# The last quarter of two weight tiles by itself, and the last outputs made in two steps

## The chip, the cores and the metric

The kernel runs on one core of one Trainium2 chip. The time is that of the device for one execution, in microseconds (us). Five engines work side by side, each through its own list of instructions in order: TensorE (PE; PEld are its weight loads), VectorE (DVE), ScalarE (ACT), GpSimd (POOL) and SyncE (SP). Transfers are issued by an engine's queue (here SP's and POOL's) and carried out by 16 DMA engines.

## What is computed

Attention with a feature map of exponentials (its output is x) is followed by a spectral mix over the sequence: the first 64 frequencies of x are multiplied with complex 512 x 512 matrices, transformed back and added to x, and a small network with ReLU is added to the sum.

```
def _moe_ref(x, w_r, w_i, w_ch):
    X = np.fft.rfft(x, axis=1)
    Y = np.zeros_like(X)
    Xr, Xi = (np.real(X[:, :n_modes]), np.imag(X[:, :n_modes]))
    Yr = np.einsum('bmd,mde->bme', Xr, w_r) - np.einsum('bmd,mde->bme', Xi, w_i)
    Yi = np.einsum('bmd,mde->bme', Xr, w_i) + np.einsum('bmd,mde->bme', Xi, w_r)
    Y[:, :n_modes] = Yr + 1j * Yi
    y = np.fft.irfft(Y, n=S, axis=1)
    u = x + y
    return (u + np.maximum(u @ w_ch, 0.0)).astype(np.float32)
```

x is 8 x 576 x 512, w_r and w_i are 64 x 512 x 512 each in float32 (134 MB together), the output is 8 x 576 x 512 in float32 (9.44 MB).

## The kernel before

**Weights.** The 64 modes stand in 8 groups of 8 (o = 0 to 7), the 512 input features in 4 groups of 128 (g = 0 to 3). One weight tile, (g, w) with w = 2 o + i, holds 8 modes by 128 features by 512 of w_r (i = 0) or w_i (i = 1). `wload` (line 348) brings it by one transfer on POOL's queue that also turns float32 into bfloat16: 2 MB are read, 1 MB is put down. In the tile, [128, 4, 2, 512], partition 2p + a holds modes 4a to 4a + 3, so index 3 of the second axis is modes 3 and 7. The tiles live in the pool `pw` of 9 buffers (line 83); `next_w` issues the next one of the list `wq`, in the order of lines 359 to 362: the groups o = 6 and 7 of g = 1 to 3 come last, and the very last are (3, 14) and (3, 15).

**Mix.** `mix` (line 472) multiplies a tile with the spectrum XT on TensorE. A matmul has 32 columns of weights (two parts, two signs and 8 batches of one mode), so four modes fill 128 output rows in PSUM: rows 0 to 31 are modes 0 and 4 of the tile (j = 0), rows 96 to 127 modes 3 and 7 (j = 3). For o = 7 the 512 output columns lie as two halves in two banks. Groups 0 to 5 are summed in `yacc`, the late groups through g = 1 to 3 in PSUM, with the part of g = 0 added from `late`.

**The end of a group.** When tile (3, 2 o + 1) is through (lines 1001 to 1058): `yst` is y of this group, 128 x 512 in bfloat16; it is transposed on TensorE, copied to `yT` and multiplied with w_ch (`wchb`) to z, copied to `zst`. Groups 0 to 6 are parked and laid out (`park`, `lay`) for the sums over many modes. `put` (line 838) copies yst and zst of groups 6 and 7 into the tile `yl`, 16 partitions at a time, twice each (128 KB a copy): for o = 6 by POOL's queue, for o = 7 by SP's.

**Sums and outputs.** `todo` is a list of closures that `fill` runs between the tiles: products x w_ch (`Channels`) and the inverse transforms of groups 0 to 6 (`Absorb`, two PSUM banks each, from the pools `pst` and `psa` of four banks each, lines 603 to 612). The 36 output pieces of 128 x 512 leave in 18 pairs (`pairs`, line 633). A pair has a side e, which ScalarE copies to `rl` (with or without ReLU; GpSimd may add x to it), and a side d in two banks (`pp`), which VectorE adds to it into `of`; one side is made of y, the other of z. A pair marked straight (third entry in the table) takes the part of group 7 from yst or zst themselves, the others take groups 6 and 7 from `yl`. `plan` (line 653) is the order of TensorE's instructions at the end, written by hand: a word has the side, then b (base: x or x w_ch by an identity matmul), s or l (the sum), the pair's name and perhaps which half. Words without a pair are marks: `until` (line 943) plays the plan up to one. A pair whose sums are all issued is added and stored by SP in the order of the table; the first one leaves in two halves.

All instructions keep the order of the program on their engine (the class InOrder), so line 37 stands for nearly all of them, and the profile is read by tile names.

Of the kernel before, what the change touches and what calls it, by code (L numbers as in the profile page):

```python
# [11 lines left out]
BF16 = mybir.dt.bfloat16  # L12
# [31 lines left out]
def kernel(  # L44
# [303 lines left out]
    def wload(g, w):  # L348
        wt = home(g, w)
        o, i = w // 2, w % 2  # L350
        w = (moe_w_r, moe_w_i)[i]
        pool.dma_start(
            wt.rearrange("p m r e -> p m (r e)"),
            w[MG * o:MG * o + MG, g * 128:(g + 1) * 128, :].rearrange(
                "m (p r) e -> p m (r e)", r=2))
        return wt
# [4 lines left out]
    order = list(wq)  # L361
    wq.remove((0, 5))
# [3 lines left out]
    def next_w(n):  # L366
        for _ in range(n):
            if wq:
                key = wq.pop(0)
                wts[key] = wload(*key)  # L370
# [101 lines left out]
    def mix(g, w, wt, XT, bank):  # L472
# [6 lines left out]
        n = 1 if w < 14 or not late else 2  # L479
        if first:  # L480
            pys[w // 2] = [bank() for _ in range(n)]
        for h, py in enumerate(pys[w // 2]):
            cols = slice(DMODEL // n * h, DMODEL // n * (h + 1))
            for r in range(2):
                for j in range(4):
                    pe.matmul(
                        py[32 * j:32 * j + 32, 0:DMODEL // n],
# [126 lines left out]
    def banks(dt=F32):  # L614
# [18 lines left out]
    pairs = {  # L633
        "00": (((0, 0), (0, 1)), True, False, True),
        "02": (((0, 2), (0, 3)), True, False, False),
        "06": (((0, 6), (0, 7)), True, True, True),
        "04": (((0, 4), (0, 5)), False, False, False),
        "34": (((3, 4), (3, 5)), False, False, True),
        "30": (((3, 0), (3, 1)), False, False, False),
        "n0": (((0, 8), (1, 8)), False, False, True),  # L640
        "14": (((1, 4), (1, 5)), False, False, False),
        "10": (((1, 0), (1, 1)), False, False, True),
        "24": (((2, 4), (2, 5)), False, False, True),
        "22": (((2, 2), (2, 3)), False, False, False),
        "32": (((3, 2), (3, 3)), False, False, True),
        "26": (((2, 6), (2, 7)), False, False, False),
        "12": (((1, 2), (1, 3)), False, False, False),
        "n1": (((2, 8), (3, 8)), False, False, False),
        "20": (((2, 0), (2, 1)), False, False, True),
# [314 lines left out]
    while mixq:  # L964
# [30 lines left out]
        if g == NG - 1 and i == 1:  # L995
# [15 lines left out]
            for h in range(2):  # L1011
                if end:
                    until(f"T{h}")
# [78 lines left out]
```

## Time and profile before

| what | value |
|---|---|
| time of three runs | 431.33 us median (430.72 to 431.49) |
| the profiled execution, its own time | 432.54 us |
| its span, first to last instruction | 430.7 us |
| mean granted TensorE clock | 0.928 |
| busy PE, DVE, ACT, POOL | 324.0, 302.4, 299.8, 123.8 us |
| read and written in HBM | 163.64 MB, 9.44 MB |
| weight transfers | 58 into wt of 1 MB, 27 us from issue to landing |
| output stores | 17 of 512 KB (4.6 us to landing), 2 of 256 KB (2.5 us) |

The span is what the profile covers; around it lies 1.84 us of the profiled execution's own time. Busy shares are averages over stages with different limits. The page's 40 slices of 10.8 us show which resource is full in which stage:

```profile
PE   1677577678787776876877767867899789985992
DMA  9999999999999999999999999999999999997697
GB/s 216 210 211 211 238 213 237 226 223 237 240 210 236 214 237 238 238 210 239 213 239 221 226 244 228 212 212 212 212 211 212 212 211 212 211 212 158 230 392 305
```

A digit is the busy share of a slice in tenths, GB/s is what the DMA engines put down.

### The profile page before, as it was taken

How to read it: one execution, taken by the hardware profiler on the slowest of the kernel's cores; microseconds unless marked ns; L12 is line 12 of the kernel's file. 1: busy time of each engine (PE TensorE's matmuls, PEld its weight loads, DVE VectorE, ACT ScalarE, POOL GpSimd, SP SyncE). 2: the span in 40 equal slices, each digit the busy share in tenths (PEclk: the TensorE clock that was granted, in tenths of full speed). 3: DMA queues.
4: the chain of work that ended last, by engine and by line, in shares of the span. 5: the costliest groups of instructions: out<-in, count | busy, mean ns of one | idle time of the engine just before them, and what ended most of it. 6: DMA issues, size and time to landing. Idle time of an engine off the chain costs nothing.

```text
span 430.7 us, 10131 instructions
## 1 busy us (share of the span) xinstructions
PE 324.0 (75%) x4208; PEld 197.8 (46%) x4255; DVE 302.4 (70%) x594; ACT 299.8 (70%) x487; POOL 123.8 (29%) x161
## 2 busy tenths in 40 slices
PE   1677577678787776876877767867899789985992
PEld 1345455446454553654645545543355333332320
DVE  6758767766677767878877878868644656972684
ACT  3787886877879779888878779766644346661872
POOL 6232132022321312321222321221012035750882
PEclk9979898889988989998988989899899999998998
DMA  9999999999999999999999999999999999997697
GB/s 216 210 211 211 238 213 237 226 223 237 240 210 236 214 237 238 238 210 239 213 239 221 226 244 228 212 212 212 212 211 212 212 211 212 211 212 158 230 392 305
DMA packets 49687, 97.71 MB, mean 227 GB/s; under 512 B 2282, under 2 KB 11626, under 8 KB 49642
## 3 DMA queue, kind: packets, MB, share of 16 engines
q0 software_dynamic: 45088, 85.27, 101.3%
q1 hardware_dynamic: 4394, 11.73, 7.2%
q8 instruction: 33, 0.54, 0.5%
q14 instruction: 12, 0.10, 0.1%
q10 hardware_dynamic: 160, 0.07, 0.1%
HBM read 163.64 MB, written 9.44 MB: 402 GB/s over the span
## 4 chain that ended last, share of the span: by engine, by line
PE 38%; ACT 28%; DVE 19%; DMA 7%; issue 5%; POOL 2%; ACTq 0%; DVEq 0%; POOLq 0%
PE one L37 14%; PE pt L37 13%; ACT AQ L37 12%; PE two L37 8%; ACT AB L37 8%; DVE m L37 7%; DMA wt<-in_moe_w_i_dram 7%; ACT qT L37 3%; ACT XT L37 3%; DVE xs L37 3%; PE pp L37 2%; DVE xw L37 2%; DVE of L37 2%; DVE mk L37 1%; DVE yacc L37 1%
## 5 line engine op out<-in xcount | busy, mean ns | idle before, releaser
L37 ACT ACTIVATE AQ<-two 128x1024 bf16<-128x1024 f32 x64 | 80.7, 1351 | 2.0 <-PE two L37 1.9
L37 ACT ACTIVATE AB<-two 128x1024 bf16<-128x1024 f32 x64 | 62.9, 1058 | 3.3 <-DVE mk L37 3.0
L37 ACT CAST xw<-pt 128x512 bf16<-128x512 f32 x54 | 31.6, 585 | 37.1 <-PE pt L37 36.3
L37 DVE TENSOR_REDUCE m<-two 128x8 f32<-128x1024 f32 x32 | 39.1, 1223 | 22.4 <-PE two L37 22.4
L37 DVE TENSOR_REDUCE mk<-two 128x8 f32<-128x1024 f32 x32 | 38.9, 1219 | 9.2 <-PE two L37 9.2
L37 PE MATMUL pt<-wchb,xT 128*128 128x512 bf16 x135 | 37.1, 388 | 8.3 <-DVE xT L37 2.4
L37 POOL DMA_DIRECT2D wt<-in_moe_w_i_dram x28 | 21.0, 751 | 76.3 <-PE pt L37 36.5
L37 PE MATMUL two<-w2blk,qT 128*128 128x256 bf16 x128 | 24.1, 322 | 24.1 <-ACT AQ L37 13.6
L37 DVE TENSOR_TENSOR va<-vn,ee 128x1152 bf16<-128x1152 f32 x32 | 42.0, 1355 | 0.0
L37 POOL DMA_DIRECT2D wt<-in_moe_w_r_dram x30 | 22.4, 747 | 55.9 <-PE one L37 28.2
L37 PEld LDWEIGHTS <-xs 128*128 128x128 bf16 x624 | 31.1, 102 | 12.7 <-issue 6.0
L37 ACT COPY qT<-one 128x512 bf16<-128x512 bf16 (+1 forms) x32 | 19.0, 642 | 23.0 <-PE one L37 22.9
L37 PEld LDWEIGHTS <-qT 128*128 128x128 bf16 x144 | 15.3, 109 | 38.9 <-issue 34.8
L37 PE MATMUL two<-mT,minus 96*128 96x512 bf16 x64 | 26.5, 414 | 2.9 <-issue 0.9
L37 POOL DMA_DIRECT2D kb<-in_k_dram x16 | 11.4, 712 | 60.1 <-PE one L37 53.4
L37 PEld LDWEIGHTS <-XT 128*32 128x32 bf16 x560 | 15.8, 148 | 28.0 <-issue 18.3
L37 DVE TENSOR_TENSOR xs<-one,rd 128x384 bf16<-128x384 f32 x48 | 26.8, 557 | 1.6
L37 PE MATMUL one<-kvz,AQ 128*128 128x65 bf16 x512 | 25.9, 203 | 1.0 <-ACT qT L37 0.8
L37 PEld LDWEIGHTS <-AQ 128*128 128x128 bf16 x512 | 23.2, 104 | 7.2 <-issue 3.0
L37 PE MATMUL one<-wt,XT 128*32 128x512 bf16 x272 | 23.8, 438 | 3.4 <-ACT XT L37 3.4
L37 POOL TENSOR_TENSOR rl<-rl,xs 128x512 f32<-128x512 f32 x18 | 20.3, 1159 | 19.3 <-ACT rl L37 18.7
L37 PE MATMUL two<-w2blk,kT 128*128 128x256 bf16 x128 | 21.1, 293 | 5.1 <-ACT AB L37 5.1
(151 smaller groups left out, 725.4 us busy)
## 6 DMA issues: line engine op xcount, KB each, us to landing
wt<-in_moe_w_r_dram POOLq DMA_DIRECT2D x30, 1024.0 KB, 26.6
wt<-in_moe_w_i_dram POOLq DMA_DIRECT2D x28, 1024.0 KB, 27.7
out_dram<-of SPq DMA_DIRECT2D x17, 512.0 KB, 4.6
vn<-in_v_dram POOLq DMA_DIRECT2D x13, 576.0 KB, 24.4
kb<-in_k_dram POOLq DMA_DIRECT2D x16, 288.0 KB, 19.2
qb<-in_q_dram POOLq DMA_DIRECT2D x16, 288.0 KB, 18.3
xs<-in_moe_w_i_dram POOLq DMA_DIRECT2D x2, 1024.0 KB, 23.0
vn<-in_v_dram SPq DMA_DIRECT2D x2, 576.0 KB, 4.7
```

The lines of the kernel that those rows point to most:

```text
L37: ins = f(*args, **kwargs)
```

## The change

- The last two tiles, (3, 14) and (3, 15), come in parts: modes 0 to 2 and 4 to 6 in two transfers of 384 KB each (one for each parity of the partitions), and at the very end of the list, modes 3 and 7 of both tiles in one transfer of 256 KB each.
- `mix` takes the modes to do. For these two tiles the main loop does j = 0 to 2, and a new function `finish` does j = 3 when the rest is there. For group 7 it uses three banks: rows 0 to 95 in two halves of the columns as before, and the rows of j = 3 in a third bank as four column blocks of 128, each in its own group of 32 rows. So a matmul of j = 3 has 128 columns.
- `finish` makes yst, yT and z of rows 0 to 95 first, puts j = 3 of tile 14 and then of tile 15 between the z matmuls, copies the third bank to `y3`, transposes it once, moves its four blocks into rows 96 to 127 of yst (two copies on VectorE, two on GpSimd), and makes z of those rows with 8 matmuls of 256 columns.
- `put` of group 6 goes to SP's queue instead of POOL's.
- Four pairs instead of three are straight (04 is new); the order of pairs, which of them use GpSimd, and the plan are new; the first three pairs are stored in halves.
- `Absorb` takes its banks from `psa` alone while group 7 holds its three banks. For the groups before 7, y is added in one instruction of 512 columns instead of two of 256, yT is one tile, and the transposes' banks are taken one after the other.

```diff
@@ -345,20 +345,29 @@
             return pw.tile([128, 4, 2, DMODEL], BF16, name="wt", tag="wt")
         return t.rearrange("p (m r e) -> p m r e", m=4, r=2)
 
-    def wload(g, w):
-        wt = home(g, w)
-        o, i = w // 2, w % 2
-        w = (moe_w_r, moe_w_i)[i]
-        pool.dma_start(
-            wt.rearrange("p m r e -> p m (r e)"),
-            w[MG * o:MG * o + MG, g * 128:(g + 1) * 128, :].rearrange(
-                "m (p r) e -> p m (r e)", r=2))
+    parted = [(NG - 1, w) for w in range(2 * NO - 2, 2 * NO)]
+
+    def wload(g, w, rest=False):
+        wt = wts[g, w] if rest else home(g, w)
+        to = wt.rearrange("p m r e -> p m (r e)")
+        src = (moe_w_r, moe_w_i)[w % 2][
+            MG * (w // 2):MG * (w // 2) + MG, g * 128:(g + 1) * 128, :].rearrange(
+                "m (p r) e -> p m (r e)", r=2)
+        if rest:
+            pool.dma_start(to[:, 3], src[:, 3::4])
+        elif (g, w) in parted:
+            for a in range(2):
+                pool.dma_start(to.rearrange("(p a) m e -> a p m e", a=2)[a, :, 0:3],
+                               src[:, 4 * a:4 * a + 3])
+        else:
+            pool.dma_start(to, src)
         return wt
 
     wts = {}
     wq = [(g, mg) for g in range(NG) for mg in range(12 if g else 2 * NO)]
     wq += [(g, 2 * o + i) for o in (6, 7) for g in range(1, NG) for i in range(2)]
     order = list(wq)
+    wq += [(*key, True) for key in parted]
     wq.remove((0, 5))
     wq.insert(1, (0, 5))
     mixq = []
@@ -367,7 +376,9 @@
         for _ in range(n):
             if wq:
                 key = wq.pop(0)
-                wts[key] = wload(*key)
+                wts[key[:2]] = wload(*key)
+                if len(key) > 2 and wq:
+                    next_w(1)
 
     scr = xs[:, 1].rearrange("p b n d -> p (b n d)").bitcast(F32)
     wpf = scr[:, 1920:2048]
@@ -469,22 +480,30 @@
                                   op0=ALU.mult, op1=ALU.add)
     pys = {}
 
-    def mix(g, w, wt, XT, bank):
+    def mix(g, w, wt, XT, bank, modes=range(4)):
 
         o, i = w // 2, w % 2
         late = g > 0 and o > 5
         first, last = i == 0 and (not late or g == 1), i == 1 and (not late or g == NG - 1)
         if late and g == 1:
             XT, o = XTb[0], o - 2
-        n = 1 if w < 14 or not late else 2
+        end = late and w >= 2 * NO - 2
         if first:
-            pys[w // 2] = [bank() for _ in range(n)]
-        for h, py in enumerate(pys[w // 2]):
-            cols = slice(DMODEL // n * h, DMODEL // n * (h + 1))
-            for r in range(2):
-                for j in range(4):
+            pys[w // 2] = [bank() for _ in range(3 if end else 1)]
+        py = pys[w // 2]
+        for r in range(2):
+            for j in modes:
+                at = py[0][32 * j:32 * j + 32]
+                parts = [(at, slice(0, DMODEL))]
+                if end and j < 3:
+                    parts = [(py[h][32 * j:32 * j + 32, 0:256], slice(256 * h, 256 * h + 256))
+                             for h in range(2)]
+                elif end:
+                    parts = [(py[2][32 * c:32 * c + 32, 0:128], slice(128 * c, 128 * c + 128))
+                             for c in range(4)]
+                for at, cols in parts:
                     pe.matmul(
-                        py[32 * j:32 * j + 32, 0:DMODEL // n],
+                        at,
                         lhsT=XT[:, i, r, :, :, :, 4 * o + j].rearrange("p t x b -> p (t x b)"),
                         rhs=wt[:, j, r, cols], start=(first and r == 0), stop=(last and r == 1),
                     )
@@ -631,31 +650,31 @@
     eye = pb.tile([128, 128], F32, name="eye", bufs=1)
 
     pairs = {
+        "02": (((0, 2), (0, 3)), True, False, False),
         "00": (((0, 0), (0, 1)), True, False, True),
+        "04": (((0, 4), (0, 5)), True, False, True),
+        "06": (((0, 6), (0, 7)), True, True, False),
+        "32": (((3, 2), (3, 3)), False, True, False),
+        "14": (((1, 4), (1, 5)), False, False, True),
...
     }
     plan = (
-        "db02 db00 mix eb020 T0 T1 es000 z0a z0b z1 es001 es020 eb06 es061 "
-        "eb021 es060 ds00 es021 ds02 eb04 el34 ds06 el04 db04 eln0 dl04 eb30 db34 el30 dl34 db30 dl30 el10 "
-        "eb14 dbn0 dln0 el14 db14 el24 dl14 eb22 db10 dl10 el32 el22 db24 dl24 eb26 db22 el20 "
-        "dl22 db32 el26 dl32 eb12 db26 dl26 el12 ebn1 db12 eln1 dl12 dbn1 dln1 el16 eb36 db20 "
-        "el36 dl20 db36 dl36 db16 dl16").split()
+        "db00 db02 mix T es000 z eb020 es020 eb021 es001 es021 es04 ds02 ds00 eb06 es06 eb32 "
+        "db04 ds04 el14 el32 db060 db061 ds06 db32 el34 dl32 eb26 db14 el26 dl14 db26 eln1 dl26 "
+        "eb30 db34 dl34 el30 eb24 db30 el24 dl30 db24 dl24 eln0 eb12 dbn1 el12 dln1 eb22 db12 "
+        "el22 dl12 db22 el36 dl22 eb10 dbn0 el10 dln0 eb16 db36 dl36 eb20 db10 el16 dl10 db16 "
+        "el20 dl16 db20 dl20").split()
     direct = [c for items, straight, _, _ in pairs.values() if straight for c in items]
 
     def inverse_tables():
@@ -766,7 +785,7 @@
             self.aside = False
 
         def all(self):
-            get = bank if full.index(self) % 2 else single
+            get = bank if full.index(self) % 2 and 7 not in pys else single
             p, q = get(), get()
             x, w = chunk(self.bp, self.n), xw[:, self.bp, self.n, :]
             rows = slice(0, 128)
@@ -839,7 +858,7 @@
         if o > 5:
             for s in copies:
                 r = 32 * s + 16 * (o - 6)
-                (pool if o == 6 else sp).dma_start(yl[r:r + 16], src)
+                sp.dma_start(yl[r:r + 16], src)
 
 
     halves = {"rl": [], "of": []}
@@ -887,7 +906,7 @@
             (bp, n), at, z = self.items[a], self.at(side, a), self.z(side)
             start = not self.based(side)
             if self.straight:
-                pe.matmul(at, lhsT=CM[n // 4][:, n % 4], rhs=zst if z else yst, start=start,
+                pe.matmul(at, lhsT=CM[n // 4][:, n % 4], rhs=ends[z], start=start,
                           stop=True)
             else:
                 r = 64 * a + 32 * z
@@ -920,7 +939,7 @@
         def store(self):
             (bp, n) = self.items[0]
             self.o = half("of")
-            parts = ([0], [1]) if self.items[0] == (0, 0) else ([0, 1],)
+            parts = ([0], [1]) if self in first else ([0, 1],)
             for p in parts:
                 a = slice(p[0], p[-1] + 1)
                 self.add(a)
@@ -939,6 +958,7 @@
 
     last = {n: Pair(*x) for n, x in pairs.items()}
     stores = list(last.values())
+    first = stores[:3]
 
     def until(mark=None):
         while plan:
@@ -960,6 +980,53 @@
                 stores.pop(0).store()
         assert mark is None
 
+    ends = []
+
+    def finish(py, yst, zst, yT):
+        E = slice(96, 128)
+        ends[:] = yst, zst
+
+        def rest(i):
+            mix(*parted[i], wts[parted[i]], XTb[parted[i][0] % 2], bank, range(3, 4))
+
+        dve.tensor_copy(yst[0:96, 0:H], py[0][0:96, 0:H])
+        act.copy(yst[0:96, H:], py[1][0:96, 0:H])
+        for h in range(2):
+            pt = bank([128, 2, 96], BF16)
+            for c in range(2):
+                at = H * h + 128 * c
+                pe.transpose(pt[:, c], yst[0:96, at:at + 128], ident_b[0:96, 0:96])
+            if h:
+                act.copy(yT[:, 2:4, 0:96], pt)
+            else:
+                dve.tensor_copy(yT[:, 0:2, 0:96], pt)
+        rest(0)
+        pz = bank()
+        for c in range(4):
+            if c == 2:
+                rest(1)
+            pe.matmul(pz[0:96], lhsT=yT[:, c, 0:96], rhs=wchb[:, c], start=(c == 0), stop=(c == 3))
+        until("T")
+        y3 = pb.tile([128, 128], BF16, name="y3", bufs=1)
+        dve.tensor_copy(y3, py[2][:, 0:128])
+        act.copy(zst[0:96], pz[0:96])
+        pt = bank([128, 4, 32], BF16)
+        pe.transpose(pt.rearrange("p c r -> p (c r)"), y3, ident_b)
+        for c in range(4):
+            (pool if c % 2 else dve).tensor_copy(
+                yst[E, 128 * c:128 * c + 128], y3[32 * c:32 * c + 32])
+        dve.tensor_copy(yT[:, :, E], pt)
+        put(yst, 7, 0, (0, 2))
+        until("z")
+        pz = [bank([128, H]) for h in range(2)]
+        for c in range(4):
+            for h in range(2):
+                pe.matmul(pz[h][64 + 32 * h:96 + 32 * h], lhsT=yT[:, c, E],
+                          rhs=wchb[:, c, H * h:H * h + H], start=(c == 0), stop=(c == 3))
+        act.copy(zst[E, H:], pz[1][E])
+        dve.tensor_copy(zst[E, 0:H], pz[0][64:96])
+        put(zst, 7, 1, (1, 3))
+
     H = DMODEL // 2
     while mixq:
         key = mixq.pop(0)
@@ -972,11 +1039,14 @@
             pst2 = ctx.enter_context(
                 tc.tile_pool(name="pst2", bufs=2, space=bass.MemoryType.PSUM))
             until("mix")
-        mix(*key, wts.pop(key), XTb[g % 2], bank)
+        mix(*key, wts[key], XTb[g % 2], bank, range(3 if key in parted else 4))
         if key == (1, 14):
             for h in range(2):
-                pe.matmul(pys[o][h][:, 0:H], lhsT=eye, rhs=late[:, 1, H * h:H * h + H],
-                          start=False, stop=False)
+                pe.matmul(pys[o][h][0:96, 0:H], lhsT=eye[:, 0:96],
+                          rhs=late[:, 1, H * h:H * h + H], start=False, stop=False)
+            for c in range(4):
+                pe.matmul(pys[o][2][32 * c:32 * c + 32, 0:128], lhsT=eye[:, 96:128],
+                          rhs=late[:, 1, 128 * c:128 * c + 128], start=False, stop=False)
         left = len(mixq)
         if left == 15:
             yall = pw.tile([128, B_, DMODEL], BF16, name="yall", tag="wt")
@@ -993,59 +1063,47 @@
         else:
             n = math.ceil(max(len(todo) - 2, 0) / max(left - 2, 1)) if left > 1 else len(todo)
         if g == NG - 1 and i == 1:
-            end = left == 0
-            py = pys.pop(o)
+            py = pys[o]
             yst = pb.tile([128, DMODEL], BF16, name="yst")
-            pt = [bank([128, 2, 128], BF16) for h in range(2)]
-            yT = [pb.tile([128, 2, 128], BF16, name=f"yT{h}") for h in range(2)]
-            if end:
-                dve.tensor_copy(yst[:, 0:H], py[0][:, 0:H])
-                act.copy(yst[:, H:], py[1][:, 0:H])
-            else:
-                for h in range(2):
-                    dve.tensor_tensor(out=yst[:, H * h:H * h + H], in0=py[0][:, H * h:H * h + H],
-                                      in1=(yacc[:, o] if o < 6 else late[:, o - 6])[:, H * h:H * h + H], op=ALU.add)
+            zst = pb.tile([128, DMODEL], BF16, name="zst")
+            yT = pb.tile([128, 4, 128], BF16, name="yT")
+            if left == 0:
+                finish(py, yst, zst, yT)
+                break
+            del pys[o]
+            dve.tensor_tensor(out=yst, in0=py[0],
+                              in1=yacc[:, o] if o < 6 else late[:, o - 6], op=ALU.add)
             put(yst, o, 0, (0, 2))
...
```

## The prediction

> **What bounds the kernel now.** I read the page's slices first: the DMA row is 9 from the start to slice 36, so up to about 390 us the weights set the pace. Then the chain of waits over the last 70 us, then stretches of the end, then the instructions in order of time. The chain (start, us, what):
>
> ```profile
> 368.01 28.03 DMA wt<-in_moe_w_i_dram
> 396.05 0.04 issue
> 396.09 5.40 PE pt L37 x33
> ```
>
> So the end hangs on the landing of the last weight tile, (3, 15), at 396.05. It was issued 28 us earlier; its issue is not the limit, the queue in front of it is. Stretches of the end (us, busy time of PE, PEld, DVE, ACT, POOL, then granted clock, DMA share, GB/s):
>
> ```profile
> 381.00:386.00 5.00, 4.08 (x32) 1.73 (x31) 3.23 (x6) 2.66 (x6) 2.30 (x2) 1.00 1.12 211
> 391.00:394.00 3.00, 2.27 (x24) 1.04 (x21) 1.34 (x2) 1.17 (x2) 0.00 (x0) 1.00 0.93 182
> 394.00:396.00 2.00, 0.59 (x3) 0.23 (x2) 0.00 (x0) 0.00 (x0) 0.00 (x0) 0.99 0.78 174
> 396.00:399.40 3.40, 3.31 (x26) 1.88 (x26) 0.93 (x3) 0.97 (x2) 0.13 (x1) 0.50 0.22 48
> 399.40:403.90 4.50, 4.31 (x23) 1.75 (x22) 2.17 (x4) 3.60 (x8) 4.09 (x4) 1.00 0.39 97
> 403.90:410.00 6.10, 5.77 (x36) 1.82 (x36) 5.68 (x6) 4.94 (x11) 5.95 (x7) 1.00 0.94 368
> 410.00:420.00 10.00, 9.38 (x59) 2.75 (x58) 8.92 (x8) 8.30 (x16) 7.83 (x7) 1.00 0.99 392
> ```
>
> Three stages. Until 396 the DMA engines are full (212 GB/s written, 424 read, since float32 comes in and bfloat16 is put down). From 396.05 to 403.9 they are nearly empty: this is the serial chain y, z, first outputs, and it begins with TensorE at half clock. From 403.9 they are full again with stores (392 GB/s): 9.44 MB at 392 GB/s are 24.1 of the last 26.8 us. So the first store's issue decides the end, and after it the DMA queue. The chain in order of time:
>
> ```profile
> 396.09 1.08 PE L37 MATMUL pt<-wt,XT 128*32 128x256 bf16 x16 [1.50 <-DMA wt<-in_moe_w_i_dram]
> 396.79 0.42 DVE L37 CAST yst<-pt 128x256 bf16<-128x256 f32 x1 [3.60 <-PE pt L37]
> 398.36 1.55 PE L37 MATMUL pt<-wchb,yT 128*128 128x384 bf16 x8
> 399.72 0.48 ACT L37 CAST zst<-pt 128x384 bf16<-128x384 f32 x1 [0.52 <-PE pt L37]
> 402.02 1.29 DVE L37 SCALAR_TENSOR_TENSOR of<-pp,rl 128x512 f32<-128x512 f32 x2 [1.79 <-POOL rl L37]
> 402.74 0.60 SPq L37 DMA_DIRECT2D out_dram<-of  x1
> ```
>
> Landing to first store: 402.74 - 396.09 = 6.65 us.
>
> **Part 1, the chain is cut.** Tiles (3, 14) and (3, 15) lose a quarter each, which comes last as 2 x 256 KB. A tile takes 5.0 us of the full queue (1.05 MB / 0.212), a quarter 1.24, so tile 15 without its quarter is there 2.5 us before the end of the stream. Rows 0 to 95 need in that time 12 matmuls of 256 columns (0.8, as 16 took 1.08 at half clock), two copies side by side (0.42), four transposes (0.63 in the same timeline) and two yT copies (0.51): 2.4 us, so they just fit, and the first two of the four 512-column z matmuls go before the last piece. What is left after the landing, with one wait of 0.06 between engines: 8 matmuls of 128 columns over four column groups and their drain (0.4), the y3 copy (0.29, as the 128x128 zst copy), one transpose (0.32), yT (0.25; two 32-row copies ahead of it on VectorE, about 0.17 each, run beside the transpose), weight load and es000 (0.37, it also waits for GpSimd's two 32-row copies, estimated at 0.26 each from its 128x1024 copy of 1.05 us), 8 z matmuls of 256 columns in two column groups (0.43), eight 512-column matmuls for pairs 02, 00 and 04 that the plan puts ahead of ds02 (8 x 0.215 = 1.7), ds02 itself (0.38), and the 0.69 us add of half a pair: 5.1 us with waits at full clock. The zst copies (0.42 and 0.37) lie beside the eight matmuls. At half clock the 512-column matmuls cost 0.43 and the whole 6.5. Before, with its 3.4 us of half clock taken out, stands at about 5.6: the 26 matmul records of that stretch, halved from where they end last (16 tile matmuls, 4 transposes, 8 z matmuls), give 1.1. So the chain is shorter by about 0.5 at full clock (5.6 to 5.1) and 0.15 at half clock (6.65 to 6.5): little, because those eight matmuls now stand between z and the first z sum.
>
> **Part 2, the first stores.** Pairs 02, 00 and 04 go out in halves (a 0.60 pitch on VectorE, 256 KB each: 0.66 us of queue), so the queue is fed without holes from its first byte. Before, 403.9 to 410 ran at 368 against up to 413 in single slices: (1 - 368/410) x 6.1 = 0.6 us of holes. All of it may be won; none if the fourth pair comes late. I take 0.6, since the sixth half is added before the queue has emptied the fourth. Three more store issues of 0.54 to 0.60 on SP lie between adds that are 0.6 apart; they just keep up.
>
> **Part 3, what is moved: the copies of yst and zst of group 6 into yl.** Before, POOL issues them, behind all weights in the same queue:
>
> ```profile
> yl<-yst POOLq DMA_DIRECT2D x2, 128.0 KB, 25.0
> yl<-zst POOLq DMA_DIRECT2D x2, 128.0 KB, 22.5
> ```
>
> Issued at 371.7 to 376, they take 25 us to land, at 396.7 to 398.2: in the empty stage, where they cost nothing. On SP they have their own queue and land ahead of the last weights, in a stage in which every byte pushes the weights back. Their cover is gone. Does a second queue take time from the first? Two windows answer, 260.0 to 263.5 (a v load on SP beside the weights) and 264.2 to 270.0 (weights alone); columns are packets, MB, share of 16 engines:
>
> ```profile
> q0 software_dynamic: 346, 0.70, 105.5%
> q1 hardware_dynamic: 42, 0.08, 7.0%
> ```
>
> ```profile
> q0 software_dynamic: 616, 1.22, 111.6%
> ```
>
> The weights fall from 106 packets per us to 99, by 7%, which is what the other queue takes: one for one. And four such copies (group 7's, 398.5 to 404.0):
>
> ```profile
> q1 hardware_dynamic: 576, 0.52, 37.8%
> ```
>
> 37.8% of 5.5 us are 2.08 us of 16 engines; a full queue shows 112%, so 1.9 us of the weight stream. From below 0.52 MB / 0.424 = 1.2 (bytes read at the weights' rate), from above 0.52 / 0.212 = 2.5. Taken: 1.8, as the share row is of the same copies. Against it stands 0.3: tile 15 lands 5.27 after tile 14 (390.82 to 396.09) instead of 4.95 (the pitch of the tiles before), because DMA engines that are through begin the copies while others still bring weights. Six transfers in place of two add their completion writes, 0.1. The landing moves by **+1.6** (0.9 to 2.5).
>
> Queues: POOL issues four transfers more of 0.75 (3 us) and four copies fewer of 0.55; behind the two last issues, which wait for a free DMA semaphore as the zst copy did at 375.99 before, stand six xw adds of 1.15 that ended at 383.6, 7 us before tile 14 lands: covered, and 7 us late if the cover goes. The queue still holds four tiles then, so the late issue starves nothing. SP issues nothing else in that stretch. The sums in stage o = 7 have four banks instead of eight; TensorE waits 1.5 to 3.2 us for each of the last two tiles, so that is free.
>
> **Sum.** Against the profiled execution (span 430.7, 432.54 in all, 1.84 around the span): +1.6 - 0.5 - 0.6 = +0.5. The median of the runs shown, 431.33, is 1.2 below it; that is about the 1.1 that the half clock cost this execution, which speaks for runs at full clock there. At full clock on both sides: 431.33 + 0.5 = **431.8 us**.
>
> The Trainium skill ("TensorE: Matmul & The Clock Gate", Part 1) says that the clock follows a free-running window of 3.4 us, at half rate after an idle one. The trace agrees in length (3.41 us from 395.97). By that rule which run meets the half clock is chance; by the row alone it always does, and the sum would be 431.33 + 0.85.
>
> **Rivals.**
> 1. *Half clock over the new chain (slower).* The clock fell at 395.97 after a window in which TensorE worked some 1.35 of 3.4 us. If it falls within 3.4 us before the last landing, the chain is 6.5 instead of 5.1: +1.4, 433.2. For it: tile 15's short work, then waits for copies. Against: more TensorE work per window than before (about 1.6 to 2.1 of 3.4). It decides if the granted clock is under 0.75 in the 3.4 us behind the landing. 0.20.
> 2. *The copies cost their upper bound*: landing +2.2 net instead of 1.6, and es000 held by GpSimd: 432.4 and up. 0.13.
> 3. *The copies are nearly hidden (faster)*: they fall on DMA engines that are ahead; the landing spread (GB/s falls from 391 on, five us before the last engine ends) says that some are. Then +0.2 in place of 1.6: 430.4. Against: 16 rows of 8 KB spread evenly. 0.24.
> 4. *The change doesn't do what it says*: a transfer counts when its last engine is through; if the pieces land with the last ones, the 2.4 us of rows 0 to 95 fall on the path: 433 or more. Against: each engine works its queue in order. 0.06.
>
> The Trainium skill ("DMA: Bandwidth & Descriptors", Anatomy of one DMA) gives each transfer about 2.0 us of fixed cost; an estimate from that page, were it paid in series, is 8 us for four more transfers. The trace speaks against it: tiles land 4.95 us apart at 212 GB/s, each 26 to 28 us after its issue, so five to six are in flight.
>
> **How the numbers follow.** A measurement of this kernel can tell 0.2%, 0.86 us, from no change (its three runs lie 0.77 apart). The forecast (0.37) has its own range 430.5 to 432.2. Rivals 1, 2 and 4 are slower (0.39), rival 3 faster (0.24). The range reaches over most of 3 and of 1: 430.0 to 433.4; left out are rival 4 and the ends of the bounds.
>
> **What would show it.** yl<-yst and yl<-zst of group 6 land a few us after SP's issue; the last weights land at 397.3 to 398.0; y3's copy begins 0.4 to 0.5 behind; first store 5.1 to 6.5 behind; stores without holes to the end. The forecast is wrong if the last landing stays under 396.8 (rival 3), if the clock is half behind it (rival 1), or if VectorE waits for pair 32 or later long enough to empty the queue.

## The result, and the profile after

| | before | after |
|---|---|---|
| median of seven executions | 430.96 us (430.57 to 431.87) | 434.69 us (433.47 to 437.54) |
| profiled execution: time, span | 432.54, 430.7 us | 435.06, 433.3 us |
| last weights landed | 396.05 | 397.59 |
| first store issued | 402.74 | 404.08 |
| first store to the end of the span | 28.0 | 29.2 |

The change made the kernel **slower by 0.87%** (95% interval of the ratio 1.006 to 1.0114), about 3.7 us. The forecast was 431.8, and its range ended at 433.4. In the two profiled executions the span is about 2.5 us longer: 1.5 up to the last landing (of weights), 0.2 less from there to the first store, 1.2 more behind it.

The chain of waits of after, from the last big weight transfer on (start, us, what):

```profile
365.23 26.18 DMA wt<-in_moe_w_r_dram
391.45 0.67 PE pt L37 x10
392.12 0.54 PE pa L37 x2
392.71 1.50 PE pa L37 x3
394.22 0.59 ACT xw L37
394.87 1.64 PE pp L37 x4
396.50 0.66 PE pt L37 x11
...
399.19 0.30 DVE y L37
399.62 0.28 POOL yst L37
...
401.74 0.55 SPq L37
402.34 4.77 DMA yl<-zst
407.16 0.39 PE pt L37
```

Two things are new against before. The chain doesn't run through the last landing any more. It leaves the weights at tile 14 (391.41) and goes through two inverse sums (pa), a copy by ScalarE and four base matmuls (pp) of 1.64 us to the mix of tile 15 (pt, 396.50), whose modes 0 to 2 had landed at 395.09. And behind z it goes through a copy into yl of 4.77 us, to a matmul at 407.16. Stretches of the end (us, busy PE, PEld, DVE, ACT, POOL, then granted clock, DMA share, GB/s):

```profile
391.00:394.00 3.00, 2.50 (x17) 1.02 (x18) 1.32 (x2) 0.59 (x1) 0.00 (x0) 0.78 0.94 176
394.00:396.00 2.00, 1.32 (x4) 0.43 (x4) 0.06 (x1) 0.59 (x1) 0.00 (x0) 0.50 0.76 141
397.60:404.10 6.50, 5.90 (x47) 2.84 (x49) 2.36 (x8) 4.18 (x9) 2.89 (x5) 1.00 0.37 70
404.10:410.00 5.90, 4.91 (x26) 1.70 (x24) 4.41 (x7) 4.09 (x9) 4.53 (x6) 1.00 0.80 257
410.00:420.00 10.00, 9.46 (x62) 2.93 (x60) 8.92 (x8) 7.74 (x15) 6.80 (x6) 1.00 0.93 377
```

TensorE's clock was at half ahead of the last landing (392.70 to 396.11) and full behind it. In the stage of stores the first 5.9 us moved 257 GB/s where before had 368, so the queue was *not* fed without holes. VectorE's adds show the hole (the second line's bracket is the idle time ahead of it, and what ended it):

```profile
403.36 3.87 DVE L37 SCALAR_TENSOR_TENSOR of<-pp,rl 128x512 f32<-128x512 f32 x6 [1.69 <-ACT rl L37]
408.62 2.36 DVE L37 TENSOR_TENSOR of<-pp,rl 128x1024 f32<-128x1024 f32 x2 [1.39 <-PE pp L37]
```

Six half adds, then 1.39 us of nothing. In TensorE's timeline of the same execution:

```profile
405.78 0.39 PE L37 MATMUL pt<-yl,CL 32*128 32x512 bf16 x3
407.16 0.39 PE L37 MATMUL pt<-yl,CL 32*128 32x512 bf16 x1 [0.99 <-DMA yl<-zst]
407.48 0.61 PE L37 MATMUL pp<-xs,ident_b 128*128 128x512 bf16 x2
```

The fourth matmul on yl waits for the late copy; the base matmuls of the next pair (pp) stand behind it.

### The profile page after: what moved, and what is told of

Same layout as the page of the kernel before. It is cut to its first block, busy times and chain, and to the rows that moved or that the text cites. A ratio compares the mean times of both kernels' runs of the same rounds, so it can differ in the third digit from the quotient of the medians.

```text
span 433.3 us, 10227 instructions
## 1 busy us (share of the span) xinstructions
PE 327.2 (76%) x4249; PEld 199.8 (46%) x4296; DVE 302.8 (70%) x592; ACT 301.0 (69%) x489; POOL 120.1 (28%) x159
## 4 chain that ended last, share of the span: by engine, by line
PE 37%; ACT 27%; DVE 20%; DMA 7%; issue 5%; POOL 1%; SPq 0%; ACTq 0%; DVEq 0%; POOLq 0%
PE one L37 13%; PE pt L37 13%; ACT AQ L37 12%; PE two L37 8%; ACT AB L37 8%; DVE m L37 8%; DMA wt<-in_moe_w_r_dram 6%; ACT qT L37 3%; ACT XT L37 3%; PE pp L37 2%; DVE xs L37 2%; DVE xw L37 2%; DVE mk L37 2%; DVE of L37 1%; DVE mT L37 1%
## 5 line engine op out<-in xcount | busy, mean ns | idle before, releaser
L37 ACT CAST xw<-pt 128x512 bf16<-128x512 f32 x47 | 27.6, 586 | 31.5 <-PE pt L37 31.0
L37 POOL DMA_DIRECT2D wt<-in_moe_w_i_dram x30 | 22.1, 738 | 85.2 <-PE one L37 36.7
L37 PE MATMUL two<-w2blk,qT 128*128 128x256 bf16 x128 | 23.0, 311 | 24.1 <-ACT AQ L37 13.6
L37 POOL DMA_DIRECT2D wt<-in_moe_w_r_dram x32 | 23.7, 740 | 54.6 <-PE one L37 21.4
L37 DVE TENSOR_TENSOR xs<-pa,xs 128x512 bf16<-128x512 f32 x25 | 16.6, 684 | 13.4 <-PE pa L37 13.4
```

The source lines that it names most:

```text
L37: ins = f(*args, **kwargs)
```

## The experiments

All ratios are against executions of the kernel before on the same chip as the run (medians 430.93 to 431.54). Since that median moves by 0.6 us between chips, differences of runs are safer by ratio than by median; 0.1% is 0.43 us. What is read from a trace is read from one execution of each run. "The wait" is the idle time of VectorE ahead of its first add of 128x1024, 1.39 in after.

| run | median us (executions) | ratio to before, 95% |
|---|---|---|
| e1 before, copies on SP | 433.28 (5) | 1.0030 to 1.0067 |
| e2 after, copies on GpSimd | 438.95 (4) | 1.0152 to 1.0194 |
| e3 before, new pairs | 431.51 (10) | 0.9990 to 1.0015 |
| e4 after, old pairs | 432.81 (10) | 1.0023 to 1.0053 |
| e5 after, fetch moved | 435.23 (5) | 1.0053 to 1.0132 |
| e6 = e4, copies held back | 434.86 (6) | 1.0030 to 1.0111 |
| e7 after, sums ahead of tile 14 | 433.97 (9) | 1.0038 to 1.0069 |
| e8 after, one pair in halves | 434.28 (10) | 1.0037 to 1.0082 |
| e9 = e4 and e7 | 433.60 (5) | 1.0035 to 1.0071 |
| e10 = e9, copies last on GpSimd | 431.26 (12) | 0.9989 to 1.0013 |
| e11 = e7, copies last on GpSimd | 432.34 (10) | 1.0019 to 1.0044 |
| e12 before, idle matmuls | 432.25 (10) | 1.0013 to 1.0044 |
| e13 after, el32 behind pair 06 | 433.33 (6) | 1.0037 to 1.0071 |
| e14 = e11 and e13 | 431.09 (12) | 0.9986 to 1.0011 |
| e15 = e14, last pair in halves | 431.54 (12) | 1.0006 to 1.0028 |

### One part alone, or undone: e1 to e4

**e1**, the copies of group 6 alone:

```diff
-                (pool if o == 6 else sp).dma_start(yl[r:r + 16], src)
+                sp.dma_start(yl[r:r + 16], src)
```

> The kernel before with one part of the change alone: group 6's four copies into yl are issued by SP in place of GpSimd. Theory (their 0.52 MB go ahead of the last weights and push them back): last weights land 397.3 to 397.8 instead of 396.05, everything behind them as before, time 431.0 + 1.5 = 432.5. Rival (the copies are hidden and the later landing of the changed kernel comes from its six transfers in place of two): landing within 0.3 of 396.05, time 431.0.

The last weights landed at 397.75, 1.7 later; the time rose by 0.49%, 2.1 us (1.3 to 2.9; by the medians 1.7). The theory holds. The DMA view of 370 to 392 shows the price, first before, then e1 (packets, MB, share of 16 engines):

```profile
q0 software_dynamic: 2331, 4.67, 111.7%
```

```profile
q0 software_dynamic: 2128, 4.22, 102.1%
q1 hardware_dynamic: 576, 0.52, 10.9%
```

The weights' queue gave up 9.6% of 22 us, 2.1 us of 16 engines, for 0.52 MB.

**e2**, the same part undone in the changed kernel (the diff of e1 turned round).

> The changed kernel with this part undone: group 6's copies on GpSimd again, behind all weights in their queue. Theory: last weights land 396.0 to 396.4, the copies at 398 to 399, time 434.7 - 1.5 = 433.2. Rival (the split itself delays the landing): landing stays at 397.3 or later, time 434.7. A third possibility: the landing comes back but the copies, now among group 7's, delay the first use of yl: time 434 to 434.7 with yl<-zst landing behind 407.

The landing came back (395.98), and yet this was the slowest kernel of all, 4.3 us above the changed one by the medians, 3.7 by the ratios. GpSimd's timeline (an issue, then what it waited for):

```profile
381.33 0.58 POOL L37 DMA_DIRECT2D yl<-yst  x1 [4.68 <-DVE xs L37]
385.94 0.55 POOL L37 DMA_DIRECT2D yl<-yst  x1 [4.03 <-DMA wt<-in_moe_w_i_dram]
386.51 1.16 POOL L37 TENSOR_TENSOR xw<-rl,xw 128x512 bf16<-128x512 f32 x1
388.11 0.53 POOL L37 DMA_DIRECT2D yl<-zst  x1 [0.43 <-issue]
389.70 0.53 POOL L37 DMA_DIRECT2D yl<-zst  x1 [1.07 <-DMA wt<-in_moe_w_r_dram]
390.24 5.60 POOL L37 TENSOR_TENSOR xw<-rl,xw 128x512 bf16<-128x512 f32 x5
```

The last two tiles now come by six transfers in place of two. The copies' issues wait for weights to land, and the xw adds behind them on GpSimd wait too; the last one ends at 395.84. ScalarE and TensorE wait for these adds, and the mix of tile 15, landed at 393.30, began at 401.05. (TensorE's clock was also at half from 387.02 to 393.84 in this execution.) None of the three expectations was right: what decides is not the transfer but the queue of GpSimd that its issue blocks. So the move to SP avoids a loss of about 4 us that the split would make, although it costs some 1.6 itself.

**e3 and e4**, the table of pairs and the plan exchanged, with the marks fitted; e3 also stores its first three pairs in halves, e4 only its first. The beginnings of the plans, e3 against before and e4 against after:

```diff
-        "db02 db00 mix eb020 T0 T1 es000 z0a z0b z1 es001 es020 ...
+        "db00 db02 mix T0 T1 es000 z0a z0b z1 eb020 es020 eb021 es001 ...
```

```diff
-        "db00 db02 mix T es000 z eb020 es020 eb021 es001 ...
+        "db02 db00 mix eb020 T es000 z es001 es020 eb06 es061 ...
```

> The kernel before with the changed kernel's pairs and plan alone (three pairs in halves, pair 32 as the fifth); the tiles, the copies and the y and z chain stay as before. Theory (after the sixth half nothing is ready, since pair 32 waits for yl<-zst; the loss of 1.3 us in the stage of stores belongs to this order): time 431.0 + 1.3 = 432.3, with a wait of VectorE over 1 us ahead of the first 128x1024 add. Rival (the prediction's: halves feed the queue without holes): 430.4. Second rival (the wait belongs to the late y and z of the changed chain): 431.0, no such wait.

> The changed kernel with the pairs and plan of before (one pair in halves, three straight pairs, pair 34 as the fourth). Theory: the wait ahead of the first 128x1024 add goes, time 434.7 - 1.3 = 433.4. First rival (the prediction's): 434.7 + 0.6 = 435.3. Second rival (the loss comes from the yl<-zst copies of 4.8 us, whatever the order): the wait only moves to another pair, time 434.7.

e3 is where before is: no gain of 0.6, and no loss either. e4 is 1.9 below the changed kernel. So the new pairs cost nothing with the old chain and about 1.9 us with the new one as it stands. VectorE in e3, then in e4:

```profile
401.00 3.87 DVE L37 SCALAR_TENSOR_TENSOR of<-pp,rl 128x512 f32<-128x512 f32 x6 [1.72 <-ACT rl L37]
405.19 2.36 DVE L37 TENSOR_TENSOR of<-pp,rl 128x1024 f32<-128x1024 f32 x2 [0.33 <-PE pp L37]
```

```profile
402.55 2.42 DVE L37 SCALAR_TENSOR_TENSOR of<-pp,rl 128x512 f32<-128x512 f32 x3 [1.89 <-PE pp L37]
404.97 1.23 DVE L37 TENSOR_TENSOR of<-pp,rl 128x1024 f32<-128x1024 f32 x1
406.41 4.86 DVE L37 SCALAR_TENSOR_TENSOR of<-pp,rl 128x1024 f32<-128x1024 f32 x4 [0.22 <-PE pp L37]
```

The wait of 1.39 is 0.33 in e3. In e4 there is none ahead of the first add of 128x1024 and 0.22 ahead of the next ones. Both executions ran at full clock from 390 to 425, and this gives the chain without the clock: first store 5.50 us behind the last landing with the old y and z chain (e3: 396.22 to 401.72), 5.52 with the new one (e4: 397.75 to 403.27).

### Why the new pairs cost only with the new chain: e5, e8, e13

**e8**, whole stores for the second and third pair:

```diff
-    first = stores[:3]
+    first = stores[:1]
```

> The changed kernel with only its first pair in halves, the second and third whole, everything else the same. Theory (halves are neutral; the loss lies in the wait for pair 32): the wait ahead of the fourth pair stays at 1.3 or more, time 434.7 within 0.4. Rival (halves empty the queue, or their three more store issues hold up SP): 434.0 or less.

434.28, 0.4 below the changed kernel, with intervals that overlap: no effect of the halves is seen. (e14 below keeps them and is level with before.) The profiled execution, at 436.67 above the median, shows what the clock can do here:

```profile
390.40:396.00 5.60, 4.06 (x19) 1.53 (x21) 1.38 (x2) 1.17 (x2) 0.00 (x0) 0.50 0.89 166
396.00:403.90 7.90, 7.35 (x51) 2.70 (x50) 1.62 (x7) 1.87 (x4) 0.81 (x3) 0.50 0.07 16
```

Half clock over the whole chain, and the first store 9.6 us behind the landing (397.21 to 406.79). The wait of 1.3 or more that was expected ahead of the fourth pair is 0.35 there, but with the first store that late it can't be compared.

**e5**, 75 idle matmuls early in groups 6 and 7, so that TensorE's next block of instructions is fetched at another time.

```diff
+        if key in ((2, 12), (2, 13), (3, 12), (1, 14), (1, 15)):
+            spin(15)
```

> The changed kernel with 75 idle matmuls of 32 columns (150 TensorE instructions with their weight loads) spread behind five weight tiles of groups 6 and 7, so that the instruction fetch that lay at 404.2 among the yl<-zst copies (16 KB, 1.88 us, one DMA engine) comes 150 instructions earlier, in the empty stage before 400. They write a bank that nothing reads. Theory (the fetch makes the last yl<-zst copy 1.0 us longer, and VectorE waits for it): yl<-zst lands at most 3.8 us after its issue, the wait ahead of the first 128x1024 add falls from 1.39 to 0.5 or less, time 434.7 - 1.0 = 433.7. Rival (the copies are slow because they follow the yl<-yst copies more closely than before, 1.48 us apart in place of 2 to 2.7): copies still 4.5 us or more, wait unchanged, time 434.7.

The DMA view behind the issue of yl<-zst (packets, MB, share), first of after (401.7 to 407.2), then of e5 (401.8 to 407.2):

```profile
q8 instruction: 1, 0.02, 2.1%
...
yl<-zst SPq DMA_DIRECT2D x2, 128.0 KB, 3.9
```

```profile
q14 instruction: 1, 0.01, 1.1%
...
yl<-zst SPq DMA_DIRECT2D x2, 128.0 KB, 4.0
```

In after, a packet of instructions took 2.1% of 16 engines for 5.5 us, 1.85 us of one engine; in e5 it is gone from this stretch. The slower of the two copies fell from 4.77 to 4.13, and the wait ahead of the first 128x1024 add from 1.39 to 0.75. So the fetch made nearly half of the wait. The theory wanted 1.0 off both and got 0.64. The time didn't fall: further on another fetch now lies among the stores, whose landings on one engine come 2 us behind the others (418.08 against 416.03), and two of five executions had a clock of 0.913. Which of these kept the time up isn't shown. The time is a miss for the theory; the copies bear it out in part.

The Trainium skill ("Runtime: NRT & Kernel Launch", Instruction fetch mechanics) says that instructions come in blocks of 16 KiB through a DMA queue of the sequencer's own and that this is mostly hidden. The trace agrees on the 16 KB packet. It isn't hidden here from a transfer that shares the DMA engine: the copy beside it took 4.77 us instead of 4.13.

**e13**, one swap in the plan:

```diff
-        "db04 ds04 el14 el32 db060 db061 ds06 db32 el34 dl32 ...
+        "db04 ds04 el14 db060 db061 ds06 el32 db32 el34 dl32 ...
```

> The changed kernel with one swap in TensorE's order: the yl products of pair 32 (el32) behind the bases and sums of pair 06 (db06, ds06) instead of ahead of them. Nothing else moves. Theory (pair 06 needs no yl at all; its add waited 1.39 only because its matmuls stand behind el32, which waits for the late yl<-zst): the wait ahead of the first 128x1024 add falls to 0.4 or less, the adds end 0.8 to 1.1 earlier, time 434.7 - 1.0 = 433.7. Rival (the wait only moves on to pair 32, whose relu and add come next): wait of 0.9 or more ahead of the second 128x1024 add, time 434.7.

433.33, 1.4 below the changed kernel, as the theory has it. TensorE, then VectorE:

```profile
406.06 0.39 PE L37 MATMUL pt<-yl,CL 32*128 32x512 bf16 x2
406.38 0.61 PE L37 MATMUL pp<-xs,ident_b 128*128 128x512 bf16 x2
```

```profile
407.53 1.22 DVE L37 TENSOR_TENSOR of<-pp,rl 128x1024 f32<-128x1024 f32 x1
408.92 1.23 DVE L37 TENSOR_TENSOR of<-pp,rl 128x1024 f32<-128x1024 f32 x1 [0.16 <-ACT rl L37]
```

Pair 06's bases now run right behind el14. No wait is left ahead of its add, and 0.16 ahead of pair 32's, although the fetch lies among the copies here as well (4.49 us). From the first store to the end of the span it is 28.1 us, against 29.2 in after and 28.0 in before. The late copy costs nothing if nothing that is needed sooner stands behind the matmul that waits for it.

How long the wait is can be read off all the traces with el32 ahead of pair 06 and three pairs in halves. The length of the last yl<-zst copy, then the wait:

| e3 | e5 | e2 | after | e11 | e7 |
|---|---|---|---|---|---|
| 3.72, 0.33 | 4.13, 0.75 | 4.54, 1.16 | 4.77, 1.39 | 4.83, 1.45 | 4.86, 1.48 |

In every one the wait is the copy's length less 3.38 or 3.39. So the same plan waits with the old chain (e3) too; its copy is only shorter. Of the 1.05 us between e3 and after, 0.64 is gone where the fetch is moved (e5). The rest goes with how closely the copies follow each other, as the rival in e5 has it: with no 16 KB fetch among them, the last copy took 4.13 where the first yl<-zst is issued 1.5 us behind the first yl<-yst (e4, e5), and 3.42 to 3.72 where it is 2.0 to 2.7 behind (before, e1, e3). No run changed that distance alone.

### The chain and the copies: e6, e7, e9 to e12

**e7**: all of `todo` is done one tile earlier, so the last two sums run ahead of tile 14.

```diff
-            n = ... if left > 1 else len(todo)
+            n = ... if left > 2 else len(todo)
```

> The changed kernel with the two xw sums that ran between tile 14 and tile 15 put ahead of tile 14, so that the base matmuls of the first pairs no longer stand behind them. Theory (the chain gained only 0.16 because the mix of tile 15, landed at 395.09, began at 396.43): that mix begins within 0.2 of its landing, y3's copy within 0.6 of the last landing, first store 5.3 to 5.7 behind it in place of 6.49, time 434.7 - 0.8 = 433.9. Rival (the chain behind the last landing is set by y3, GpSimd and the eight matmuls, not by when rows 0 to 95 are ready): first store still 6.3 or more behind, time 434.7.

```profile
395.11 0.67 PE L37 MATMUL pt<-wt,XT 128*32 128x256 bf16 x12 [2.13 <-DMA wt<-in_moe_w_i_dram]
395.83 0.42 DVE L37 CAST yst<-pt 96x256 bf16<-96x256 f32 x1 [5.71 <-PE pt L37]
...
397.98 0.29 DVE L37 CAST y<-pt 128x128 bf16<-128x128 f32 x1 [1.12 <-PE pt L37]
```

The mix starts at its landing, y3's copy 0.44 behind the last one (397.54), the first store 5.32 behind it; time 433.97. This execution had no half clock between 390 and 428, so the edit and the clock aren't parted by it alone. In e9, where the clock fell at 395.60, the mix also began 0.05 behind its landing.

**e6**: e4, and group 6's copies on SP held back. `give` stands in `finish` behind the copy of rows 0 to 95 into yst.

```diff
+    def give():
+        for src, z, copies in held:
+            dve.tensor_copy(src[0:1, 0:1], src[0:1, 0:1])
+            for s in copies:
+                sp.dma_start(yl[32 * s:32 * s + 16], src)
```

> The changed kernel with the pairs of before and group 6's four copies still on SP, but held back until rows 0 to 95 of the last y are copied (one element of their sources is rewritten there, which the copies wait for). Theory (copies ahead of the weights cost 1.5 to 1.7): last weights land at 396.1 to 396.5 in place of 397.75, time 432.8 - 1.5 = 431.3. Rival (held back, they push the last quarter tiles or delay group 7's copies as much): landing 397 or later, or yl<-zst later than 3.9 us behind its issue; time 432.4 or more.

A miss, by the rival's second half: the landing was 395.65, but eight copies now followed each other, the last two landed 5.9 and 6.1 us behind their issue, and TensorE stood at the first use of yl for 0.94 and 0.82 us. After that the clock fell to half (404.06 to 410.89). What the copies and what the clock cost isn't parted: the six executions lie between 431.55 and 436.81.

**e9** is e4 with e7's edit; **e10** adds group 6's copies on GpSimd, behind its last xw add; **e11** is the same with the change's own pairs.

```diff
+            if left == 1:
+                give()
```

Here `give` issues the four copies by `pool.dma_start`.

> The changed kernel with the pairs of before (e4) and the two xw sums ahead of tile 14 (e7). Theory (the two losses are separate): mix of tile 15 within 0.2 of its landing, first store at most 5.6 behind the last landing, wait ahead of the first 128x1024 add under 0.3, time 432.8 - 0.7 = 432.1. Rival (the sums ahead of tile 14 only helped because of the clock of that execution): 432.8.

> e9 with group 6's copies on GpSimd again, but issued behind its last xw add, so that waiting for a free DMA semaphore holds no add. Theory (copies ahead of the weights cost 1.5; in e2 GpSimd's held adds cost the rest): last weights land 396.1 to 396.5, copies by 399, no wait of TensorE for xw ahead of tile 15, time 432.1 - 1.5 = 430.6, which is below the kernel before by 0.9. First rival (late copies take their time from group 7's, as in e6): yl<-zst of group 7 over 5 us, time 432 to 434. Second rival (issues still late and GpSimd's copies of y3 held): es000 waits over 1 us for GpSimd, time 432.

> The changed kernel with its own pairs, the two xw sums ahead of tile 14 (e7) and group 6's copies on GpSimd behind its last add. Theory: last weights 396.1 to 396.5, time 434.0 - 1.5 = 432.5, of which 1.9 above e10 are the pairs' (wait for pair 32 over 1 us, fetch of instructions among the yl<-zst copies). Rival (the pairs cost nothing of their own, as in e3): 430.6 like e10.

e9 is a miss: 433.6 in five executions from 432.33 to 434.71. Its profiled one ran at half clock from 395.60 to 402.42, with the first store 7.30 behind the landing. It is no faster than e4, and by ratio level with e7, which has the new pairs: so what the sums ahead of tile 14 gain, and what the pairs cost, isn't the same in every combination. e10 has the landing at 396.09 and the copies by 397.92, and its time, 431.26, is that of before: the copies ahead of the weights were worth 2.3 us there, and 1.6 between e7 and e11 (0.9 by the ratios). But 430.6 was expected, so nothing of the split's gain is seen. GpSimd's issues wait in e10 as in e2, and hold no add any more:

```profile
379.88 3.43 POOL L37 TENSOR_TENSOR xw<-rl,xw 128x512 bf16<-128x512 f32 x3
383.22 0.59 POOL L37 DMA_DIRECT2D yl<-yst  x1
385.87 0.55 POOL L37 DMA_DIRECT2D yl<-yst  x1 [2.06 <-DMA wt<-in_moe_w_i_dram]
```

**e12** was to tell how many executions of before meet the half clock.

```diff
             until("mix")
+            warm(8)
+        elif len(mixq) == 1:
+            warm(14)
```

> The kernel before with 14 idle matmuls of 256 columns ahead of tile 14 and 8 ahead of tile 15, into columns that nothing reads, so that TensorE is busy through the waits for the last two tiles. Theory of the prediction (most executions of before run this chain at full clock; the half clock of its profiled execution, 395.97 to 399.38, cost it 1.1): no half clock between 388 and 402, first store 5.4 to 5.7 behind the landing, median time unchanged within 0.3. Rival (the half clock is met in most executions): median 0.7 to 1.1 below before. Second rival (idle matmuls delay tile 15): mix over 0.2 behind its landing, time 0.3 to 1 above.

It doesn't: in the profiled execution TensorE was late already, the idle matmuls pushed tile 15's mix to 398.64, 2.4 us behind its landing (396.22), and the time rose by 0.3%, as the second rival has it. The question is open.

### All three mended: e14, e15

e14 is e11 with e13's swap: sums ahead of tile 14, copies on GpSimd behind its last add, el32 behind pair 06. e15 on top of it:

```diff
-    first = stores[:3]
+    first = stores[:3] + stores[-1:]
```

> The same swap on top of e11 (xw sums ahead of tile 14, group 6's copies on GpSimd behind its last add). Theory: 432.3 - 1.0 = 431.3, level with the kernel before and with e10; nothing then remains of the changed kernel's loss, and of its gain either. Rival (pairs of the change cost more than this wait): 432.0 or more. Second rival (with the wait gone the shorter chain shows): 430.6 or less.

> e14 with the last pair also added and stored in halves. Theory (the stores are bound by VectorE's adds, and the last transfer alone lies behind them): last landing 2.7 behind the last add instead of 3.3, time 431.1 - 0.6 = 430.5, below the kernel before by 0.6. Rival (the queue is full at the end and one DMA engine lags): 431.1.

e14 is level with before, and 1.25 us below e11, which differs by the swap alone (the intervals lie apart). e15 is no gain: its last landing comes 3.3 us behind the last add, as in e14, and its last two half stores land 0.67 us apart, the last two whole ones of e14 1.27 (412 GB/s). So even the last stores stand in a full queue. No version beat the kernel before.

## Why the prediction was wrong

**The step that failed** is in part 2: "the queue is fed without holes from its first byte ... none if the fourth pair comes late". The bound of "none" was wrong: a late fourth pair is a loss, +1.2 us behind the first store in the two spans instead of -0.6. The sixth half was indeed added early, but pair 06 was late, because TensorE's order has el32 ahead of its bases, and el32 waits for yl<-zst. The last section of the forecast named a wait of VectorE for pair 32; the pair that waited was 06, which needs no yl. The wait has no price in the forecast at the place where it falls: in TensorE's queue, behind an instruction that needs the last DMA of the chain. Moving el32 alone took off 1.4 us (e13) and 1.25 us (e14 against e11). And where it was mended, the gain of 0.6 wasn't to be had: from the first store to the end e14 takes 27.5 us, and e4, which has the old pairs, 27.5 too; e3 27.7, before 28.0.

**The loss, located.** From the changed kernel to e14, the steps are sums ahead of tile 14 (e7), copies behind the weights (e11) and el32 behind pair 06 (e14). By the medians they are worth 0.7, 1.6 and 1.25 us, by the ratios 1.5, 0.9 and 1.4; together that is 3.6 or 3.8, all of the 3.7. The sum and the last step are shown. How the rest splits between the first two is open to 0.8 us, and the first by itself is not shown, since the same edit gained nothing in e9.

**Part 3 was right.** Copies ahead of the last weights, one for one from their stream: +1.6 (0.9 to 2.5) expected, +1.5 in after, +1.7 in e1, and 1.8 between the landings of e7 and e11 (397.54, 395.77). Rival 3, copies nearly hidden, falls, and so does rival 2, their upper bound (+2.2). No run measures the 0.1 for completion writes by itself. The forecast's remark on GpSimd's queue held as well, for SP; e2 shows the other side of it.

**Part 1 gained little or nothing.** At full clock the chain was to fall from 5.6 to 5.1. Measured at full clock: 5.50 with the old chain (e3), 5.52 with the new one (e4), and 5.32 with the new one and the sums ahead (e7, e11). So 0.2 of the 0.5 came at best. The steps are as many as before (copy, transpose, copy, z matmuls, copy, sums, relu, add); they became shorter in columns, not fewer, and es000 waits 0.52 us for GpSimd's two copies, which the forecast held covered. (The plan has seven matmuls ahead of ds02, not the eight of the forecast: 401.14 to 402.66 in after, 1.5 us for 1.7. VectorE's two 32-row copies took 0.22 each, not 0.17.) In the profiled execution the chain took 6.49 with the clock full behind the landing. That is close to the number given for half clock (6.5), by another way, so that agreement is luck: the half clock lay ahead of the landing, and it delayed the work that should have been done by then.

**Rival 1** (half clock, 433.2) is therefore half right: not over the new chain, but over the two sums and four base matmuls ahead of it. These lie between tiles 14 and 15, which the forecast hadn't looked at as a step: the cover for the mix of rows 0 to 95 was counted from its landing, not from when TensorE is free. How many executions of before and after meet the half clock, and so how much of the 3.7 it makes, stays open. **Rival 4** falls: the pieces landed 2.5 us ahead of the last one (395.09, 397.59).

## What to carry to other kernels

A chain that is cut into a part made ahead and a short rest gains only if the engine is free when the early part lands; list what stands ahead of it in that engine's order, at half clock too. Where each engine works in order, a late transfer costs what is queued behind the first instruction that waits for it, so put work that doesn't need the transfer ahead. A change of issuing queue is priced on both sides: what the transfer takes from the stream it now runs beside, and what its issue holds up on the engine that issues it.

## What was not expected of the hardware

- A transfer's issue on GpSimd waited 4.03 us for weights to land (e2) and stopped the adds behind it. With the same four issues behind the last add and the sums ahead of tile 14 the kernel took 432.34 in place of 438.95 (e11); the two edits aren't parted there.
- A 16 KB packet of instructions took 1.85 us of one DMA engine, and the copy beside it was 0.6 us longer (4.77 against 4.13). It depends on where it falls: where it began 2.6 and 2.9 us behind the copy's issue (e9, e10), the copy took 3.43 and 3.42.
- The clock's falls lie elsewhere in each execution: in 17 profiled executions the clock was at half somewhere between 387 and 411 in ten, in pieces of 3.41 to 13.65 us. TensorE was busy for 1.20 of the 3.40 us ahead of the fall in after, and for 1.36 of 3.41 in before, and its last longer pauses ahead of the falls were 3.00 (after) and 3.19 and 1.50 us (before), so the clock fell here without 3.4 us of idleness. The Trainium skill ("TensorE: Matmul & The Clock Gate", Part 1) gives an idle window of 3.4 us as the condition; the length agrees with the 3.41 here, the idleness does not.
